# Attention scores of 32 tiles: two products over 64 rows into two PSUM banks in place of a block-diagonal product over 128 rows

## Chip, cores and metric

One core of one Trainium2 chip runs the whole program. The metric is the device time of one execution in microseconds (us). Of the kernel before there are three timed runs; of one more execution there is a profile, read below.

## What is computed

A pooled attention and two feed-forward layers with different activations, one after the other, in float32:

```python
# q, k, v: [B=8, H=8, S=576, D=64]
k_p = k.reshape(B, H, 72, 8, D).mean(axis=3)         # the same for v
scores = (1 / sqrt(D)) * q @ k_p.T                   # [B, H, 576, 72]
attn = softmax(scores)                               # along the 72
x = (attn @ v_p), heads side by side                 # [4608, 512]
h = x @ w_in                                         # [4608, 2048]
g = where(h >= 1, h, where(h <= -1, 0, (h + 1)**2 / 4))
x2 = g @ w_out                                       # [4608, 512]
out = relu(x2 @ w_in2)**2 @ w_out2                   # [4608, 512]
```

## The kernel before

The 4608 tokens are cut into 36 tiles of 128 (the attention's unit) and 9 blocks of 512 (the unit of the feed-forward layers). A batch has 576 tokens, which is four and a half tiles, so tiles 4, 13, 22 and 31 hold the end of one batch and the start of the next; they are called crossing tiles here. The eight heads of a tile are four pairs (`NP`), and a pair's 2 x 64 dimensions fill 128 rows.

**The attention of a tile** goes through units, each a few TensorE (PE) instructions and an evacuation. For tiles 4 to 35:

- `unit_q` gives the transposed queries `qT` (128 rows of a pair's dimensions, 4 pairs, 128 tokens); from tile 8 on the DVE transposes them and PE has no part in it.
- `unit_s` makes the scores, in two units per tile, `("s", t, 0)` and `("s", t, 1)`, each of two pairs. `kbd` holds the pooled keys of a batch as a block diagonal: rows 0 to 63 hold the first head of the pair in columns 0 to 71, rows 64 to 127 the second head in columns 72 to 143, and the rest is zero. One product of 128 rows and 144 columns (line 371) thus gives both heads of a pair. A crossing tile takes two products per pair, one for each batch, with 64 tokens each. The evacuation takes the maximum (line 389) and subtracts it (line 396) on the DVE; the exponential (line 411) runs on ACT a little later.
- `norm` (lines 429 to 440) sums and scales; the result goes out to DRAM and comes back in another order (`do_stores`, `fetch`), and the DVE turns it (`turn`, line 477) into `aT`.
- `unit_x` multiplies `aT` with the pooled values (line 487) into `px`; ACT and the DVE evacuate it as `xhi` (line 499) and `xlo` (line 500).

A float32 product appears as two passes on PE, each with its own weight load (PEld).

**The feed-forward work** runs in steps. Step `s` is `gemm1(s)` (12 products of 512 columns, line 665), then `gemm2(s - 2)` (12 of 512 columns, line 737; in the first ten steps 4 float32 ones, line 726), with the evacuations and weight splits on ACT and the DVE.

**What sets the order.** The table `slots` gives each unit a place: slot `2s` is between `gemm1(s)` and `gemm2(s - 2)`, slot `2s + 1` behind `gemm2`. For tiles 8 to 35, four steps apart, `("s", t, 0)` stands at `2c`, `("s", t, 1)` at `2c + 2` (one step later) and `("x", t)` at `2c + 11`; for tiles 4 to 7 the two score units stand at `2c` and `2c + 1`, in the same step. The recording layer then orders the instructions of each engine.

**PSUM.** Outside the opening, `bank` takes from the pool `ps_a`, which has two banks. All units of the attention share these two in turn; a unit waits until the bank's earlier user is evacuated. The products of `gemm1` and `gemm2` have banks of their own.

Of the kernel before, what the change touches and what calls it, by code (L numbers as in the profile page):

```python
# [10 lines left out]
F32 = mybir.dt.float32  # L11
# [3 lines left out]
AF = mybir.ActivationFunctionType  # L15
ALU = mybir.AluOpType
AX = mybir.AxisListType
# [16 lines left out]
def pooled_attention_moe_moe(  # L34
# [11 lines left out]
    nc = tc.nc  # L46
    B, H, S, D = q.shape
# [3 lines left out]
    SP = S // POOL  # L51
    P = 128
    NP = H // 2
# [6 lines left out]
    exp_scale = 1.0 / (POOL * float(D) ** 0.5)  # L60
# [17 lines left out]
    at = attn.enter_context(tc.tile_pool(name="at", bufs=2))  # L78
# [10 lines left out]
    kbd = [ac.tile([P, NP, 2 * SP], F32, name=f"kbd{i}") for i in range(2)]  # L89
# [10 lines left out]
    def runs(t0, n):  # L100
        done = 0
        while done < n:
            b, s = divmod(t0 + done, S)
            step = min(n - done, S - s)
            yield done, step, b, s
            done += step
# [119 lines left out]


    q_t, kv_t, kp, vp, qT, pn_t, p_d, z_t, aT = {}, {}, {}, {}, {}, {}, {}, {}, {}
    x_t, sums = {}, {}
    early, later, norms, stores, fetches, fetched, turns = [], [], [], [], [], [], []  # L230

    def bank(shape, name):

        n = early[-1] % 8 if early else 0
        if n >= 4:
            return ps_acc.tile(shape, F32, tag=f"acc{n - 4}", name=name)
        if n % 2:
            return ps_h.tile(shape, F32, tag="h", name=name)
        return ps_a.tile(shape, F32, tag="a", name=name)
# [102 lines left out]
    def unit_q(t):  # L342
# [20 lines left out]

        return evac

    def unit_s(t, g):
        pss = bank([P, 2, 2 * SP], "pss")
        for i in range(2):
            p = 2 * g + i
            for off, n, b, _ in runs(t * P, P):  # L370
                nc.tensor.matmul(  # L371
                    out=pss[off:off + n, i, :], lhsT=qT[t][:, p, off:off + n], rhs=kbd[b % 2][:, p, :],
                    start=True, stop=True,
                )
        if g == 0:
            if t == 3:
                pn = [gp.tile([P, H // 2, SP], F32, tag="gl", name="pn") for _ in range(2)]
            else:
                pn = early_pn(t) if t < 2 else at.tile([P, H, SP], F32, tag="pn", name="pn", bufs=1)
                pn = [pn[:, 0:H // 2, :], pn[:, H // 2:, :], pn]  # L380
            pn_t[t] = pn, at.tile([P, H, 1], F32, tag="mx", name="mx", bufs=4)
            if t in ON_ACT:
                sums[t] = at.tile([P, H, 1], F32, tag="sm", name="sm", bufs=4)
        pn, mx = pn_t[t][0][g], pn_t[t][1]
        h = slice(4 * g, 4 * g + 4)
        s4 = pss.rearrange("p i (e s) -> p (i e) s", e=2)

        def evac():
            nc.vector.tensor_reduce(out=mx[:, h, :], in_=s4, axis=AX.X, op=ALU.max)
            if t in ON_ACT:  # L390
                nc.vector.tensor_scalar(
                    out=mx[:, h, :], in0=mx[:, h, :], scalar1=-exp_scale, scalar2=None, op0=ALU.mult
                )
                later.append(exp)
                return
            nc.vector.tensor_tensor(
                out=pn, in0=s4, in1=mx[:, h, :].to_broadcast([P, 4, SP]), op=ALU.subtract
            )
            later.append(exp)

        def exp():
            if t in ON_ACT:
                for i in range(4 * g, 4 * g + 4):
                    nc.scalar.activation(
                        out=pn[:, i - 4 * g, :], in_=s4[:, i - 4 * g, :], func=AF.Exp, scale=exp_scale, bias=mx[:, i, :],
                        accum_out=sums[t][:, i, :],
                    )
                if g == 1:
                    norms.append(t)
                return  # L410
            nc.scalar.activation(out=pn, in_=pn, func=AF.Exp, scale=exp_scale)
            if g == 1:
                norms.append(t)

        return evac

    def early_pn(t):
        flat = pad[t].rearrange("p n h c -> p (n h c)")
        return flat[:, 0:H * SP].rearrange("p (h s) -> p h s", h=H)
# [87 lines left out]
    TB0 = TB // P  # L507
# [6 lines left out]
    for t in range(TB0, NTILE):  # L514
# [10 lines left out]
        if t in first_tile:  # L525
            b = first_tile.index(t)
# [36 lines left out]
    def unit(u):  # L563
        if u[0] == "k":
            b, p = u[1:]
            pool_to(b * 2 * NP + p + 2)
            return unit_k(b, p)
        if u[0] == "v":
            b, p = u[1:]
            pool_to(b * 2 * NP + NP + p + 2)  # L570
            return unit_v(b, p)
        if u[0] == "q":
            load_q_to(u[1] + (1 if u[1] >= TB0 else 0))
            return unit_q(u[1])
        if u[0] == "s":
            return unit_s(*u[1:])
        if u[0] == "p":
            return unit_p(*u[1:])
        b = max(r[2] for r in runs(u[1] * P, P))
        pool_to((b + 1) * 2 * NP)  # L580
        return unit_x(u[1])
# [295 lines left out]
    for u in before:  # L877
        op, args = u.rstrip("0123456789,"), [int(i) for i in u.lstrip(ascii_lowercase).split(",") if i]
# [220 lines left out]
    for n, u in enumerate(units):  # L1099
        kind, b, i, g = u  # L1100
# [52 lines left out]
```

## Time and profile before

| | |
|---|---|
| three timed runs | 1636.98, 1637.51, 1638.68 us |
| their median | 1637.51 us |
| span of the profiled execution (first to last instruction) | 1636.0 us |
| the rest of the median around that span | 1.51 us |
| PE busy | 1612.2 us (99% of the span), 7824 instructions |
| weight loads (PEld) busy | 1311.6 us (80%) |
| DVE busy | 1263.0 us (77%) |
| ACT busy | 893.5 us (55%) |
| chain that ended last | PE 91%, DVE 4%, DMA 2% |

The profiled execution has no time of its own beside its span; the median of the runs lies 1.51 us above it. A busy PE counts each product from its start to the end of its last column on the way out, so products that overlap are counted once, and the distance between the starts of two products tells more of what one costs than its duration does.

### The profile page before, as it was taken

The page shows a single profiled execution, that of the slowest core. Times are in us where ns is not written, and L with a number is a line of the kernel's source. Part 1 is how long each engine was busy: PE and PEld are TensorE (multiplying, and loading weights), DVE is VectorE, ACT ScalarE, POOL GpSimd, SP SyncE. Part 2 cuts the span into 40 slices and gives each one's busy share as a digit, 9 for nine tenths or more (in the row PEclk, how much of TensorE's full clock was granted, in tenths as well). Part 3 has the DMA queues.
Part 4 walks back from the last instruction along what each step waited for, and adds up shares of the span by engine and source line. Part 5 has one row for each costly group of instructions (what it writes and reads, how often), then busy time and mean ns, then how long its engine had stood idle before and what let it go on. Part 6 is the DMA issues. An engine that isn't in the chain of part 4 may idle for free.

```text
span 1636.0 us, 23310 instructions
## 1 busy us (share of the span) xinstructions
PE 1612.2 (99%) x7824; PEld 1311.6 (80%) x7824; DVE 1263.0 (77%) x2228; ACT 893.5 (55%) x1610; POOL 106.6 (7%) x75
## 2 busy tenths in 40 slices
PE   7999999999999999999999999999999999999998
PEld 6757888888878888888888888888888888888886
DVE  6998889998898999998884542579558855975585
ACT  6665556666666666666675532345335533553353
POOL 1442000011001000000100000000000000000000
PEclk9999999999999999999999999999999999999999
DMA  9664335544455554544470384667776776768675
GB/s 246 191 193 124 107 69 170 163 157 139 148 145 156 155 144 134 171 142 151 141 258 7 103 277 147 194 218 207 195 254 219 209 235 208 211 198 245 194 206 129
DMA packets 280518, 284.69 MB, mean 174 GB/s; under 512 B 154960, under 2 KB 183632, under 8 KB 280400
## 3 DMA queue, kind: packets, MB, share of 16 engines
q1 hardware_dynamic: 280400, 283.21, 58.0%
q8 instruction: 62, 1.02, 0.3%
q14 instruction: 56, 0.46, 0.1%
HBM read 218.10 MB, written 65.01 MB: 173 GB/s over the span
## 4 chain that ended last, share of the span: by engine, by line
PE 91%; DVE 4%; DMA 2%; ACT 1%; issue 1%; SPq 1%; POOL 0%; DVEq 0%; ACTq 0%; POOLq 0%
PE ph L665 25%; PE acc L737 25%; PE dp L1011 11%; PE cp L1002 10%; PE dq L1011 5%; PE cr L1002 5%; PE dr L1011 3%; PE cq L1002 2%; PE pss L371 2%; PE px L487 2%; DMA w<-w2i 1%; PE acc L726 1%; DVE wi L155 0%; DMA kv<-in_k_dram 0%; SPq L1068 0%
## 5 line engine op out<-in xcount | busy, mean ns | idle before, releaser
L665 PE MATMUL ph<-xhi,wihi 128*128 128x512 f32 x576 | 230.4, 400 | 1.4 <-ACT xhi L499 1.4
L665 PE MATMUL ph<-xlo,wihi 128*128 128x512 f32 x576 | 225.4, 391 | 0.0
L665 PE MATMUL ph<-xhi,wilo 128*128 128x512 f32 x576 | 225.2, 391 | 0.0
L959 ACT ACTIVATE gh<-g 128x512 fp32r<-128x512 f32 x224 | 139.5, 630 | 152.1 <-DVE g L1028 48.0
L737 PE MATMUL acc<-gh,wohi 128*128 128x512 f32 x536 | 215.8, 403 | 0.0
L737 PE MATMUL acc<-gl,wohi 128*128 128x512 f32 x536 | 209.5, 391 | 0.0
L737 PE MATMUL acc<-gh,wolo 128*128 128x512 f32 x536 | 209.0, 390 | 0.0
L767 DVE TENSOR_TENSOR gl<-g,gh 128x512 fp32r<-128x512 f32 x224 | 151.1, 686 | 47.6 <-ACT gh L959 46.2
L1002 PE MATMUL cp<-x,w 128*128 128x512 f32 x768 | 186.2, 390 | 0.2
L1002 PEld LDWEIGHTS cp<-x,w 128*128 128x128 f32 x768 | 143.9, 188 | 31.3 <-ACT s L1024 1.4
L1011 PE MATMUL dp<-gh,w 128*128 128x512 f32 x512 | 161.5, 389 | 0.0
L219 ACT ACTIVATE wihi<-wi 128x512 fp32r<-128x512 f32 x144 | 90.4, 628 | 125.3 <-PE ph L665 122.3
L223 DVE TENSOR_TENSOR wilo<-wi,wihi 128x512 fp32r<-128x512 f32 x144 | 105.3, 731 | 49.0 <-ACT wihi L219 47.7
L665 PEld LDWEIGHTS ph<-xhi,wihi 128*128 128x128 f32 x576 | 108.4, 188 | 28.5 <-issue 3.1
L665 PEld LDWEIGHTS ph<-xhi,wilo 128*128 128x128 f32 x576 | 108.5, 188 | 23.3 <-issue 0.2
L665 PEld LDWEIGHTS ph<-xlo,wihi 128*128 128x128 f32 x576 | 108.5, 188 | 22.0 <-issue 0.5
L700 ACT ACTIVATE gh<-g 128x512 fp32r<-128x512 f32 x134 | 84.2, 629 | 68.7 <-DVE g L698 68.1
L1024 ACT ACTIVATE s<-cp 128x512 f32<-128x512 f32 x96 | 57.1, 595 | 117.9 <-PE cp L1002 117.1
L706 DVE TENSOR_TENSOR gl<-g,gh 128x512 fp32r<-128x512 f32 x150 | 104.8, 698 | 18.6 <-ACT gh L700 15.9
L737 PEld LDWEIGHTS acc<-gl,wohi 128*128 128x128 f32 x536 | 100.6, 188 | 22.4
L737 PEld LDWEIGHTS acc<-gh,wohi 128*128 128x128 f32 x536 | 100.7, 188 | 20.3 <-issue 1.0
L737 PEld LDWEIGHTS acc<-gh,wolo 128*128 128x128 f32 x536 | 100.8, 188 | 19.5
(142 smaller groups left out, 3006.8 us busy)
## 6 DMA issues: line engine op xcount, KB each, us to landing
w<-w2i SPq DMA_DIRECT2D x224, 256.0 KB
w<-w2o SPq DMA_DIRECT2D x224, 256.0 KB
w2i<-cb SPq DMA_DIRECT2D x32, 512.0 KB
w2o<-cb SPq DMA_DIRECT2D x32, 512.0 KB
st<-in_moe_w_out_dram SPq DMA_DIRECT2D x31, 512.0 KB
st<-in_moe_w_in_dram SPq DMA_DIRECT2D x29, 512.0 KB
pd<-pad SPq DMA_DIRECT2D x32, 384.0 KB
z<-pd SPq DMA_DIRECT2D x96, 128.0 KB
```

Of the source, the lines that this page charges most:

```text
L219: nc.scalar.activation(out=hi, in_=src, func=AF.Copy)
L223: eng.tensor_tensor(out=lo, in0=src, in1=hi.bitcast(F32), op=ALU.subtract)
L371: nc.tensor.matmul(out=pss[off:off + n, i, :], lhsT=qT[t][:, p, off:off + n], rhs=kbd[b % 2][:, p, :], start=True, stop=True,)
L665: nc.tensor.matmul(out=ph, lhsT=a[:, kk % a.shape[1], :], rhs=c[:, kk, :], start=(i == 0), stop=(i == 3 * KD - 1))
L700: act(out=gh, in_=g, func=AF.Copy)
L706: nc.vector.tensor_tensor(out=gl, in0=g, in1=gh.bitcast(F32), op=ALU.subtract)
L737: nc.tensor.matmul(out=o, lhsT=lhsT, rhs=rhs, start=(f == 0 and x == 0), stop=(f == KF - 1 and x == 2),)
L767: tt(out=out, in0=a, in1=b, op=ALU.subtract)
L959: act(out=hi, in_=a, func=AF.Copy)
L1002: nc.tensor.matmul(out=out[0], lhsT=w[:, a, k, :], rhs=xq[b, i][c][:, k, :], start=(n == 0 and i in (1, 2, 7)), stop=(n == 5), skip_group_ ...
L1011: nc.tensor.matmul(out=out[d], lhsT=w[:, a, d, :], rhs=x[c], start=(g == 0 and n == 0 and i in (1, 2, 7, 4)), stop=(g == NG - 1 and n == 2 ...
L1024: act(out=snaps[key], in_=a, func=AF.Copy)
```

## The change

For tiles 4 to 35, `unit_s` hands over to a new function, `unit_rows`. Its first call (`e == 0`) takes both banks of `ps_a` and issues the products of all four pairs: for each pair and each batch one product over rows 0 to 63 (first head, into the first bank) and one over rows 64 to 127 (second head, into the second bank), each with 72 columns. The zero blocks of `kbd` are no longer read. The evacuation of a call takes one bank, with the heads of one row half; its output is strided. The second call (`e == 1`) issues no products and evacuates the other bank. Tiles 0 to 3, `slots` and all the rest stay.

```diff
+    def unit_rows(t, e):
+        if e == 0:
+            halves_s[t] = [bank([P, NP, SP], "pss") for _ in range(2)]
+            for p in range(NP):
+                for off, n, b, _ in runs(t * P, P):
+                    for i, o in enumerate(halves_s[t]):
+                        d = slice(i * D, (i + 1) * D)
+                        nc.tensor.matmul(
+                            out=o[off:off + n, p, :], lhsT=qT[t][d, p, off:off + n],
+                            rhs=kbd[b % 2][d, p, i * SP:(i + 1) * SP], start=True, stop=True,
+                        )
+            pn = at.tile([P, H, SP], F32, tag="pn", name="pn", bufs=1)
+            pn_t[t] = [None, None, pn], at.tile([P, H, 1], F32, tag="mx", name="mx", bufs=4)
+        src = halves_s[t][e]
+        pn, mx = (a.rearrange("p (i e) s -> p e i s", e=2)[:, e] for a in (pn_t[t][0][2], pn_t[t][1]))
+        if e == 1:
+            halves_s.pop(t)
+
+        def evac():
+            nc.vector.tensor_reduce(out=mx, in_=src, axis=AX.X, op=ALU.max)
+            nc.vector.tensor_tensor(out=pn, in0=src, in1=mx.to_broadcast([P, NP, SP]), op=ALU.subtract)
+            later.append(exp)
+
+        def exp():
+            nc.scalar.activation(out=pn, in_=pn, func=AF.Exp, scale=exp_scale)
+            if e == 1:
+                norms.append(t)
+
+        return evac
+
     def unit_s(t, g):
+        if t >= TB0:
+            return unit_rows(t, g)
         pss = bank([P, 2, 2 * SP], "pss")
```

Lines behind the new function stand 32 further down in the changed kernel: 665 is 697 there, 737 is 769 and 500 is 532.

How this moves instructions, at three places. **PE, step 24** (the first score unit of tile 11; `ph` is `gemm1`, `acc` is `gemm2`, `pss` the scores). Before:

```order
L665 MATMUL ph<-xhi,wihi 128x512
L665 MATMUL ph<-xlo,wihi 128x512
L665 MATMUL ph<-xhi,wilo 128x512
L371 MATMUL pss<-kbd_118,qT 128x144 x2
L737 MATMUL acc_1874<-gh,wohi 128x512
L737 MATMUL acc_1874<-gh,wolo 128x512
L737 MATMUL acc_1874<-gl,wohi 128x512
```

Now:

```order
L697 MATMUL ph<-xhi,wihi 128x512
L697 MATMUL ph<-xlo,wihi 128x512
L697 MATMUL ph<-xhi,wilo 128x512
L373 MATMUL pss<-kbd_118,qT 128x72 x8
L769 MATMUL acc_1902<-gh,wohi 128x512
L769 MATMUL acc_1902<-gh,wolo 128x512
L769 MATMUL acc_1902<-gl,wohi 128x512
```

Eight products of 72 columns, of the two row halves by turns, stand where two of 144 stood. **PE, step 25** (where the second score unit of tile 11 stood). Before:

```order
L665 MATMUL ph<-xhi,wihi 128x512
L665 MATMUL ph<-xlo,wihi 128x512
L665 MATMUL ph<-xhi,wilo 128x512
L371 MATMUL pss<-kbd_118,qT 128x144 x2
L737 MATMUL acc_1874<-gh,wohi 128x512
L737 MATMUL acc_1874<-gh,wolo 128x512
L737 MATMUL acc_1874<-gl,wohi 128x512
```

Now:

```order
L697 MATMUL ph<-xhi,wihi 128x512
L697 MATMUL ph<-xlo,wihi 128x512
L697 MATMUL ph<-xhi,wilo 128x512
L769 MATMUL acc_1902<-gh,wohi 128x512
L769 MATMUL acc_1902<-gh,wolo 128x512
L769 MATMUL acc_1902<-gl,wohi 128x512
```

`gemm2` follows `gemm1` with nothing between them. **DVE, about step 8** (the rows up to `xlo`, the evacuation of tile 4's `px`, and behind it; `kv` and `kp` pool the keys, `wi` and `wo` are weights under conversion). Before:

```order
L297 TENSOR_TENSOR kv<-kv 72x2x256
L223 TENSOR_TENSOR wilo<-wi_898,wihi 128x512
L698 SCALAR_TENSOR_TENSOR gw<-ph,u 128x512
L297 TENSOR_TENSOR kv<-kv 72x2x128
L158 TENSOR_SCALAR wi_1162<-wi_1162 128x512
L298 TENSOR_TENSOR kp<-kv 72x128
L161 SCALAR_TENSOR_TENSOR wi_1162<-st,wi_1162 128x512
L155 TENSOR_SCALAR wo_1254<-wo_1254 128x512
L158 TENSOR_SCALAR wo_1254<-wo_1254 128x512
L161 SCALAR_TENSOR_TENSOR wo_1254<-st,wo_1254 128x512
L500 TENSOR_TENSOR xlo<-px,xhi 128x4x128
```

Now:

```order
L155 TENSOR_SCALAR wi_1178<-wi_1178 128x512
L158 TENSOR_SCALAR wi_1178<-wi_1178 128x512
L730 SCALAR_TENSOR_TENSOR gw<-ph,u 128x512
L161 SCALAR_TENSOR_TENSOR wi_1178<-st,wi_1178 128x512
L155 TENSOR_SCALAR wo_1270<-wo_1270 128x512
L158 TENSOR_SCALAR wo_1270<-wo_1270 128x512
L161 SCALAR_TENSOR_TENSOR wo_1270<-st,wo_1270 128x512
L532 TENSOR_TENSOR xlo<-px,xhi 128x4x128
L223 TENSOR_TENSOR wolo<-wo_1270,wohi 128x512
L509 STREAM_TRANSPOSE aT<-z 96x1024
L223 TENSOR_TENSOR wilo<-wi_971,wihi 128x512
L385 TENSOR_REDUCE mx<-pss 128x4 x2
```

The three pooling instructions that stood ahead of `xlo` stand behind it now.

## Rows read from the trace of the kernel before

**Rows 1.** The page: busy time by engine, and the chain that ended last.

```profile
PE 1612.2 (99%) x7824; PEld 1311.6 (80%) x7824; DVE 1263.0 (77%) x2228; ACT 893.5 (55%) x1610; POOL 106.6 (7%) x75
PE 91%; DVE 4%; DMA 2%; ACT 1%; issue 1%; SPq 1%; POOL 0%; DVEq 0%; ACTq 0%; POOLq 0%
```

**Rows 2.** Busy time in two stretches: length, PE, PEld, DVE, ACT, POOL, PEclk, DMA.

```profile
41.00:164.00 123.00, 118.28 (x674) 83.44 (x673) 117.11 (x205) 75.95 (x143) 46.17 (x28) 1.00 0.60 169
164.00:800.00 636.00, 636.00 (x3238) 519.48 (x3237) 569.76 (x1097) 408.94 (x748) 46.87 (x28) 1.00 0.48 144
```

**Rows 3.** Timeline of PE, tiles 25 and 26: start, duration, line, count.

```profile
549.65 0.65 PE L371 MATMUL pss<-kbd,qT 128*128 128x144 f32 x4
...
565.58 0.39 PE L665 MATMUL ph<-xhi,wihi 128*128 128x512 f32 x1
...
571.02 0.39 PE L665 MATMUL ph<-xhi,wihi 128*128 128x512 f32 x1
...
573.74 0.65 PE L371 MATMUL pss<-kbd,qT 128*128 128x144 f32 x4
579.72 0.65 PE L371 MATMUL pss<-kbd,qT 128*128 128x144 f32 x4
```

**Rows 4.** Timeline of PE, the two score units of crossing tile 13.

```profile
258.23 0.71 PE L371 MATMUL pss<-kbd,qT 128*64 128x144 f32 x8
...
264.57 0.71 PE L371 MATMUL pss<-kbd,qT 128*64 128x144 f32 x8
```

**Rows 5.** Timeline of PE, a `px` unit between regular products.

```profile
582.75 0.39 PE L737 MATMUL acc<-gl,wohi 128*128 128x512 f32 x1
583.07 1.09 PE L487 MATMUL px<-aT,vp 72*64 72x128 f32 x16
584.10 0.50 PE L665 MATMUL ph<-xhi,wihi 128*128 128x512 f32 x1
584.43 0.40 PE L665 MATMUL ph<-xlo,wihi 128*128 128x512 f32 x1
```

**Rows 6.** Timeline of the weight loads (PEld) there.

```profile
583.07 0.85 PEld L487 LDWEIGHTS px<-aT,vp 72*64 72x64 f32 x16 [0.35 <-issue]
584.09 0.19 PEld L665 LDWEIGHTS ph<-xhi,wihi 128*128 128x128 f32 x1 [0.17 <-issue]
584.20 0.19 PEld L665 LDWEIGHTS ph<-xlo,wihi 128*128 128x128 f32 x1
```

**Rows 7.** Groups by line and form: count, busy us, mean ns.

```profile
L371 PEld LDWEIGHTS pss<-kbd,qT 128*128 128x128 f32 x256 | 39.8, 193 | 7.4 <-DVE xlo L500 1.8 <-issue 0.7 <-ACT qT L362 0.4
L371 PEld LDWEIGHTS pss<-kbd,qT 128*64 128x64 f32 x64 | 3.7, 136 | 4.4 <-issue 3.3 <-ACT kbd L319 0.7 <-ACT pn L411 0.4
```

**Rows 8.** Timeline of PE, 32 passes of 72 columns in two column halves.

```profile
57.76 1.22 PE L309 MATMUL pk<-ident,kv 72*64 72x72 f32 x32
58.91 0.50 PE L665 MATMUL ph<-xhi,wilo 128*128 128x512 f32 x1
```

**Rows 9.** Groups by line and form: a score unit's maximum on the DVE.

```profile
L389 DVE TENSOR_REDUCE mx<-pss 128x4 f32<-128x288 f32 x72 | 32.3, 449 | 3.0 <-PE pss L371 2.9
```

**Rows 10.** Timeline of PE, then of DVE, around the scores of tile 6.

```profile
103.19 0.65 PE L371 MATMUL pss<-kbd,qT 128*128 128x144 f32 x4
103.68 3.60 PE L726 MATMUL acc<-gw,wo 128*128 128x512 f32 x8
108.21 0.76 PE L371 MATMUL pss<-kbd,qT 128*128 128x144 f32 x4 [0.93 <-DVE xlo L500]
...
112.99 0.30 PE L355 MATMUL pq<-ident,q 128*128 128x128 f32 x1 [1.28 <-issue]
102.15 1.38 DVE L298 TENSOR_TENSOR kp<-kv 72x128 f32<-72x128 f32 x1
...
107.47 0.68 DVE L500 TENSOR_TENSOR xlo<-px,xhi 128x512 fp32r<-128x512 f32 x1
```

**Rows 11.** Waits of PE between 41 and 164 us: total us, times, longest.

```profile
PE px L487 <- DVE aT L477: 1.3, 2, 1.1
```

More of the change, by code (lines that the diff above doesn't have):

```diff
@@ L228, in pooled_attention_moe_moe @@
     q_t, kv_t, kp, vp, qT, pn_t, p_d, z_t, aT = {}, {}, {}, {}, {}, {}, {}, {}, {}
-    x_t, sums = {}, {}
+    x_t, sums, halves_s = {}, {}, {}
     early, later, norms, stores, fetches, fetched, turns = [], [], [], [], [], [], []
```

## Prediction

> **What bounds the kernel.** The page comes first: PE is busy for 99% of the span and makes 91% of the chain that ended last [rows 1]. The scores lie in the first half, so the second view is busy time by stretch. From 164 to 800 us PE is busy in 636.00 of 636.00 us: it waits for nothing, and what the change adds to PE there, or takes off, is added to the end. From 41 to 164 us PE has 4.7 us of idle time and the DVE is busy in 117.11 of 123 [rows 2]; there both engines are near the bound and waits decide. The third view is the timeline of PE, where distances between starts give prices.
>
> A step without any unit takes 571.02 - 565.58 = 5.44 us (24 products, 0.227 each). From the first score unit of tile 26 to its second is 5.98, so **a score unit costs 0.54**. Tile to tile takes 573.74 - 549.65 = 24.09, that is four steps (21.76), two score units (1.08) and one `px` unit, which so costs 1.25 [rows 3]. In a crossing tile a score unit costs 264.57 - 258.23 - 5.44 = 0.90 [rows 4]. A tile's scores thus cost 1.08, or 1.80 in a crossing tile.
>
> **Where the price of a unit on half the array comes from.** `px` is the nearest relative of the new unit: 16 passes that run by twos on two halves of the array, column halves there, row halves in the change. Three things make its 1.25. Its first load comes 0.32 after the last regular product's start in place of 0.23: nothing is loaded ahead, PE empties first. From its first load to the next regular load is 1.02, with 0.17 of idle at the end, in which PE empties again; the rest, 0.85, is 8 pairs of passes at 0.107. Then 0.11 for a weight load that nothing covers [rows 5, 6]. The score units of regular tiles pay none of this: they are full-array products, and their loads run ahead.
>
> **The change, part by part.**
>
> *Removed:* two score units per tile, 1.08 regular, 1.80 crossing.
>
> *Added:* one unit of 16 passes (8 products, two passes each), by twos on the two row halves. A pass streams 72 columns: 32 such passes in pairs took 58.91 - 57.76 = 1.15, less 0.17 for emptying, which is 0.061 per pair [rows 8]. But each pass wants its own load of 128 columns, and two loads that follow each other at once stand 0.11 apart [rows 6]; 64 columns take 57 ns less [rows 7], so a load goes by columns, about 0.83 ns each. Before, a load of 0.107 hid under a stream of 0.12 (144 columns); now it is longer than the stream of 0.061 and sets the pace. How loads of two row halves stand to each other no row shows. From below: they run side by side, as those of two column halves do, and a pair costs 0.107, or at best the stream's 0.061. From above: one after the other, 0.214. I take 0.107, since the column halves are the nearest row. The unit is then `px` over again, 8 pairs at 0.107 and the same two emptyings: **1.25, against 1.08: +0.17 for each of 28 regular tiles, +4.8**.
>
> The Trainium skill speaks against the change at this point: "TensorE: Matmul & The Clock Gate", section LDWEIGHTS, says that a load goes by its columns alone, and that one of 32 rows takes as long as one of 128. By that halving the rows saves nothing on a load, and the sum stays as it is; no row here has a load of 64 rows.
>
> *Crossing tiles* 4, 13, 22 and 31: loads of 64 columns (0.057) and streams of 72 (0.061), on four quarters. With all four side by side 8 slots at 0.061 make 0.49 in place of `px`'s 0.86, so 1.25 - 0.37 = 0.88 in place of 1.80: -0.92 for each of 4 tiles, **-3.7**.
>
> *Evacuation:* the same two maxima, subtractions and exponentials per tile, of the same sizes. The DVE now has both maxima in one step, 0.45 us and a subtraction earlier than before [rows 9]. It is busy in 90% of that stretch and PE waited for it nowhere [rows 2]; I cost this at nothing. Without that cover it would be at most 0.9 per tile, 25 us in all, and `g` and `gl` would come late for `gemm2`.
>
> *Waits in the steady stretch:* the unit wants both banks of `ps_a` at once. Their last users are the scores of the tile before and the `px` unit of two tiles before, some two steps (11 us) earlier; I cost this at nothing.
>
> *Waits in the early stretch.* In tiles 4 to 7 the units stand closer. At tile 6 PE reaches the scores at 103.19; the bank that `px` of tile 4 holds comes free with `xlo` at 107.47 + 0.68 = 108.15. Before, the second unit alone needed it, with 3.60 of `gemm2` ahead of it, and PE waited 0.93. Now the second product needs it and `gemm2` is queued behind: with the same `xlo` PE waits about 4.8, 3.9 more. Against this: the pooling of keys is moved behind `xlo`, and its last instruction alone took 1.38; the wait of 1.28 at 112.99, for the bank of the scores, falls on a later PE [rows 10]; so do the 1.3 of waits for `aT` [rows 11]. From +3.9 down to 3.9 - 1.38 - 1.28 - 1.3 = -0.1, and below that to -1.3, if the wait for the bank doesn't grow. I take **+1.0**, nearer to the lower end, since three rows pull that way.
>
> *The sum:* 4.8 - 3.7 + 1.0 = **+2.1**. On the profiled span of 1636.0 that is 1638.1; the median of the runs lies 1.51 above the span, so **1639.6**. By its bounds (a pair between 0.102 and 0.112, which is 1.1 either way; early waits between -1.3 and +3.9) this case goes from 1636.2 to 1643.6. A measurement of this kernel can tell about 0.2%, 3.3 us; the forecast is within it.
>
> **Rivals.**
>
> *One after the other (slower).* Place: the loads of the 28 regular units. If the two row halves load through one door by turns, a pair costs 0.214, the unit 2.11, +1.03 x 28 = +28.8; a crossing unit 8 x 0.122 = 0.98, so 1.37, -0.43 x 4 = -1.7; with +1.0 for the waits **1665.6**. For it: halves of columns have separate columns, halves of rows share them. Against it: loads and products of column halves go side by side without loss. It decides early: from a pair of 0.112 on the change is slower by over 0.2%.
>
> *No load ahead (slower).* If a half can't load its next weights while it multiplies, a pair costs 0.107 + 0.061 = 0.168, the unit 1.73, +18.2; a crossing unit 8 x 0.118 = 0.94, so 1.33, -1.9; with the waits **1654.8**. Against it: `px` loads under its products; its pairs would cost 0.16 otherwise.
>
> *The stream alone counts (faster).* If loads of 64 rows are short, or hide, a pair costs 0.061 and the unit 0.88: -0.20 x 28 = -5.6, crossing -3.7, waits +1.0: **1629.3**. About the same comes out if the row halves need no emptying. Against it: the loads' 0.11 and the idle 0.17 [rows 6]. The Trainium skill has this as a rule: "TensorEngine Tiling (Array Packing)", section Theoretical Speedup, gives up to twice the speed where the contraction is 64 or less. Halving the 8 passes of 0.12 of a tile's two units gives the same 0.48. The traces bear it out for the streams alone, so its chance is small.
>
> *The change does not do what it says:* if PE treats the halves as full-array products, with no pairs, that is the first rival's price less the emptyings, and shares its chance.
>
> **How the numbers follow.** Side by side at the load's pace: 0.58, of which 0.40 within 0.2%, 0.13 slower, 0.05 faster. One after the other: 0.16. No load ahead: 0.08. The stream alone: 0.12. Early waits outside their bounds: 0.06 (0.02 within, 0.03 slower, 0.01 faster). So faster 0.18, within 0.2% 0.42, slower 0.40. The range takes in the first, the third and the fourth case, 1629 to 1655, and leaves out the second.
>
> **What would show it.** Right: in the changed profile the 16 passes of a unit start by twos, 0.107 apart, with 0.17 of idle loads behind them; tile to tile takes about 24.26 in place of 24.09, and crossing tiles 0.9 less than before; PE stays busy throughout from 164 to 800. Wrong: starts one by one, pairs of 0.06 or 0.17, loads that start while PE still streams the products before the unit, or waits of PE for the DVE in the steady stretch. A longer wait for `xlo` at tile 6 belongs to the forecast; one of more than 5 us does not.

## The result, and the profile after

The changed kernel takes 1650.77 us (median of four runs, 1649.55 to 1652.80) against 1638.10 for the kernel before (four runs, 1636.98 to 1639.27): **1.0068 times as long, 95% interval 1.0055 to 1.0082**. The two medians lie 12.7 us apart, 0.77%, which that interval takes in. The forecast was 1639.6, within 0.2% of no change. The time lies inside the stated range, but 7 us above the upper end of the likeliest case (1643.6), and nearer to a rival's figure (1654.8) whose mechanism did not happen.

The profiled execution took 1651.62 (span 1649.8). In the changed kernel the lines behind the new function are 32 higher: the scores are line 373, `px` 519, `xlo` 532, `gemm1` 697, `gemm2` 769 and 758. Busy time by stretch first, beside [rows 2], and three short windows of the early stretch (columns as there; PEclk is the third from the end):

```profile
41.00:164.00 123.00, 117.40 (x696) 81.27 (x695) 116.03 (x199) 73.19 (x137) 41.01 (x29) 0.96 0.58 169
164.00:800.00 636.00, 632.52 (x3439) 512.07 (x3438) 563.41 (x1091) 402.68 (x744) 49.05 (x28) 1.00 0.48 142
...
105.00:110.00 5.00, 2.49 (x18) 2.20 (x18) 3.43 (x5) 1.25 (x3) 2.56 (x2) 0.82 0.85 227
110.00:115.00 5.00, 5.00 (x7) 1.90 (x7) 5.00 (x11) 4.06 (x9) 0.00 (x0) 0.50 0.18 29
115.00:120.00 5.00, 5.00 (x22) 3.48 (x21) 5.00 (x12) 2.47 (x5) 1.34 (x1) 1.00 0.47 140
```

Two things are new. From 164 to 800 us PE is idle for 3.5 us, where it never was, and the early stretch has a mean clock of 0.96, with 0.50 from 110 to 115: TensorE ran there at 1.2 GHz in place of 2.4. The waits of PE (total us, times, longest) name the places:

```profile
PE pss L373 <- ACT kbd L319: 3.4, 4, 1.3
PE pss L373 <- DVE xlo L532: 2.5, 1, 2.5
PE pq L355 <- issue: 1.9, 1, 1.9
```

**The price of the unit** is read where nothing waits: PE's timeline around a regular tile, the weight loads there (and all loads of regular units as a group: count, busy us, mean ns), and PE at crossing tile 31.

```profile
584.83 0.39 PE L697 MATMUL ph<-xhi,wilo 128*128 128x512 f32 x1
585.15 1.11 PE L373 MATMUL pss<-kbd,qT 64*128 64x72 f32 x16
586.20 0.50 PE L769 MATMUL acc<-gh,wohi 128*128 128x512 f32 x1
586.53 0.39 PE L769 MATMUL acc<-gh,wolo 128*128 128x512 f32 x1
```

```profile
585.15 0.97 PEld L373 LDWEIGHTS pss<-kbd,qT 64*128 64x128 f32 x16 [0.35 <-PE ph L697]
586.20 0.19 PEld L769 LDWEIGHTS acc<-gh,wohi 128*128 128x128 f32 x1
...
L373 PEld LDWEIGHTS pss<-kbd,qT 64*128 64x128 f32 x448 | 28.7, 190 | 13.6 <-PE ph L697 7.8 <-DVE xlo L532 2.7 <-issue 1.4
```

```profile
707.59 0.39 PE L697 MATMUL ph<-xhi,wilo 128*128 128x512 f32 x1
707.90 0.73 PE L373 MATMUL pss<-kbd,qT 64*64 64x72 f32 x32
708.57 0.50 PE L769 MATMUL acc<-gh,wohi 128*128 128x512 f32 x1
708.91 0.40 PE L769 MATMUL acc<-gh,wolo 128*128 128x512 f32 x1
```

From the regular product before to the second one behind, 586.53 - 584.83 = 1.70; without the unit it would be 2 x 0.227, so the unit costs **1.25**, as forecast. Its 16 loads start by twos, 6 ns apart: eight pairs in 0.97 us, the last load being 0.19 long, are (0.97 - 0.19) / 7 = 0.111 apart. The crossing unit costs 708.91 - 707.59 - 0.45 = 0.87, forecast 0.88. Tile to tile takes 24.28 where nothing waits:

```profile
191.27 1.11 PE L373 MATMUL pss<-kbd,qT 64*128 64x72 f32 x16
...
215.55 1.11 PE L373 MATMUL pss<-kbd,qT 64*128 64x72 f32 x16
```

That is +0.19 on the 24.09 of [rows 3]; +0.17 was forecast. A crossing tile gives back 0.9.

**The early stretch**, PE's timeline at tile 6, beside [rows 10]:

```profile
105.01 0.44 PE L373 MATMUL pss<-kbd,qT 64*128 64x72 f32 x2
107.96 1.79 PE L373 MATMUL pss<-kbd,qT 64*128 64x72 f32 x14 [2.51 <-DVE xlo L532]
109.68 6.34 PE L758 MATMUL acc<-gw,wo 128*128 128x512 f32 x8
```

The first two passes run, then PE waits 2.51 us for the second bank. Behind that the granted clock is at its lower level, and the eight `gemm2` passes take 6.34 us, in place of 3.60 [rows 10]. The wait at `pq` of tile 5 has no releaser in the view (`issue`); it ends at 64.01, 0.1 us after the first of these two subtractions on the DVE, which empties the first bank of tile 4's scores:

```profile
63.46 0.81 DVE L386 TENSOR_TENSOR pn<-pss,mx 128x288 f32<-128x288 f32 x2
```

**The steady stretch**, PE at tiles 18 and 22 (three of the four waits; the fourth, 0.47, is at tile 13):

```profile
386.91 0.44 PE L373 MATMUL pss<-kbd,qT 64*128 64x72 f32 x2
388.07 1.11 PE L373 MATMUL pss<-kbd,qT 64*128 64x72 f32 x14 [0.72 <-ACT kbd L319]
...
486.71 0.34 PE L373 MATMUL pss<-kbd,qT 64*64 64x72 f32 x2 [0.97 <-ACT kbd L319]
488.33 0.72 PE L373 MATMUL pss<-kbd,qT 64*64 64x72 f32 x30 [1.28 <-ACT kbd L319]
```

Tiles 13, 18 and 22 are the first to use a new batch's keys (so are 4, 9, 27 and 31; of these only 27 lost time here, 0.46 us with 0.03 of waiting). These come through two `k` units at slots `2c - 2` and `2c - 1`, and ACT copies each into `kbd` (lines 318 and 319). Before, pairs 2 and 3 were wanted only at `2c + 2`, one step later; the one unit wants all four at `2c`. The kernel before used that step: at tile 18 its last copy ended at 380.25, after the first score unit had started (the second started at 385.79).

```profile
379.96 0.29 ACT L319 ACTIVATE kbd<-pk 64x144 f32<-64x144 f32 x1
379.81 0.65 PE L371 MATMUL pss<-kbd,qT 128*128 128x144 f32 x4
```

In the changed kernel, ACT at tile 22 shows why the copies are late (first the last of the PE products that they copy, line 314):

```profile
482.63 0.29 PE L314 MATMUL pk<-ident,kp 72*128 72x72 f32 x2
...
480.04 0.63 ACT L174 ACTIVATE cb<-z 128x512 fp32r<-128x512 f32 x1 [3.45 <-POOL z L164]
...
484.03 0.63 ACT L174 ACTIVATE cb<-z 128x512 fp32r<-128x512 f32 x1 [1.24 <-DVE z L201]
...
486.09 0.27 ACT L318 ACTIVATE kbd<-pk 64x144 f32<-64x144 f32 x1
...
487.99 0.28 ACT L319 ACTIVATE kbd<-pk 64x144 f32<-64x144 f32 x1
```

The products were done at 482.92, their copies ran at 487.69 and 487.99, behind what stands before them in ACT's order. A conversion of second-layer weights (`cb`) had held ACT for 3.45 us until POOL was done, another for 1.24; what stood behind them came late, the copies of `kbd` with it.

**Three places on the way.** The start of three `px` units divides the span: tile 0 (in the opening), tile 9 (end of the close tiles) and tile 35 (the last). In the kernel before they start at 27.25, 194.76 and 824.54 us, in the changed one at 28.23, 200.71 and 837.18. The changed kernel is thus 0.98 late at the first, loses 4.97 to the second (the *early shift*) and 6.69 to the third (the *steady shift*); what follows adds 1.2. The 0.98 is no effect of the change: E4 and E12 below, which alter nothing that early, are 1.26 and 1.28 late there.

### The profile page after: what moved, and what is told of

Same layout as the page of the kernel before. It is cut to its first block, busy times and chain, and to the rows that moved or that the text cites. A ratio compares the mean times of both kernels' runs of the same rounds, so it can differ in the third digit from the quotient of the medians.

```text
span 1649.8 us, 23897 instructions
## 1 busy us (share of the span) xinstructions
PE 1620.5 (98%) x8112; PEld 1312.4 (80%) x8112; DVE 1260.6 (76%) x2228; ACT 889.5 (54%) x1610; POOL 102.9 (6%) x75
## 4 chain that ended last, share of the span: by engine, by line
PE 83%; DVE 8%; DMA 3%; ACT 2%; issue 1%; SPq 1%; POOL 1%; DVEq 0%; POOLq 0%; ACTq 0%
PE ph L697 22%; PE acc L769 21%; PE dp L1043 11%; PE cp L1034 10%; PE dq L1043 5%; PE cr L1034 5%; PE dr L1043 3%; PE cq L1034 2%; PE px L519 2%; PE pss L373 2%; PE acc L758 1%; DMA kv<-in_k_dram 1%; POOL z L164 1%; SPq L255 1%; DMA st<-in_moe_w_in_dram 1%
## 5 line engine op out<-in xcount | busy, mean ns | idle before, releaser
L769 PE MATMUL acc<-gh,wohi 128*128 128x512 f32 x536 | 212.2, 396 | 0.0
L799 DVE TENSOR_TENSOR gl<-g,gh 128x512 fp32r<-128x512 f32 x224 | 151.5, 688 | 47.8 <-ACT gh L991 46.2
L223 DVE TENSOR_TENSOR wilo<-wi,wihi 128x512 fp32r<-128x512 f32 x144 | 99.9, 694 | 38.7 <-ACT wihi L219 38.3
L738 DVE TENSOR_TENSOR gl<-g,gh 128x512 fp32r<-128x512 f32 x150 | 108.1, 721 | 25.4 <-ACT gh L732 22.9
```

The costliest lines, as they stand in the source:

```text
L223: eng.tensor_tensor(out=lo, in0=src, in1=hi.bitcast(F32), op=ALU.subtract)
L738: nc.vector.tensor_tensor(out=gl, in0=g, in1=gh.bitcast(F32), op=ALU.subtract)
L769: nc.tensor.matmul(out=o, lhsT=lhsT, rhs=rhs, start=(f == 0 and x == 0), stop=(f == KF - 1 and x == 2),)
L799: tt(out=out, in0=a, in1=b, op=ALU.subtract)
```

## The experiments

The theory: the price of the units is near the forecast, some 2 us, and the rest is waits that come with *one unit per tile*, early for the second bank, later for `kbd`. Rivals: the rows themselves bring waits and clock; the DVE is what is waited for. Each run has its ratio to the kernel before with the 95% interval, and the two shifts of its profile as defined above. Where the text gives a ratio in us, it is its distance from 1 (or from another ratio) times 1638.

| run | ratio | early shift, us | steady shift, us |
|---|---|---|---|
| E1 early_old | 1.0040 (1.0025 to 1.0056) | +2.61 | +5.24 |
| E2 k_earlier | 1.0053 (1.0037 to 1.0070) | +4.96 | +1.59 |
| E3 both | 1.0022 (1.0012 to 1.0031) | +3.32 | +1.59 |
| E4 cross_only | 0.9984 (0.9975 to 0.9993) | +0.04 | -2.66 |
| E5 before_k_earlier | 1.0004 (0.9995 to 1.0013) | +1.65 | 0.00 |
| E6 early_only | 1.0044 (1.0032 to 1.0056) | +6.72 | 0.00 |
| E7 merge_alone | 1.0017 (1.0008 to 1.0026) | +9.54 | -1.81 |
| E7b merge_late | 0.9996 (0.9987 to 1.0005) | +2.39 | -1.81 |
| E8 halves_in_turn | 1.0100 (1.0086 to 1.0114) | +2.92 | +13.79 |
| E10 tile6_later | 1.0059 (1.0046 to 1.0073) | +5.81 | +2.16 |
| E11 change_again | 1.0081 (1.0065 to 1.0098) | +4.89 | +4.70 |
| E12 best_of_both | 0.9981 (0.9971 to 0.9990) | -0.03 | -3.54 |

The early shift of one profile is good to some 2 us only: E5 alters nothing there and shows +1.65 (its rows, further down, say why). The steady shift repeats to a hundredth where nothing waits.

**E2, the keys earlier.**

```diff
-            todo.update({2 * c - 2 + i // 2: ("k", b, i) for i in (0, 2)})
+            todo.update({2 * c - 2 - (t > 9) + i // 2: ("k", b, i) for i in (0, 2)})
```

> The change, with the two k units of batches 3 to 7 (tiles 13 to 31) one slot earlier (2c-3 and 2c-2 in place of 2c-2 and 2c-1). Theory: the four waits of the scores for kbd (5.1 us over a bare unit) go, as all four pairs are evacuated half a step before the unit; the time is the changed kernel's less 4.5 to 5.5 us, some 1645.5, with units of 0.87 us (crossing) and 1.25 us at tiles 13, 18, 22, 27. Rival: what is waited for is the DVE, whose two maxima and two subtractions come closer together, and kbd is only the last of several; then the waits stay under another name and the time changes by under 1.5 us.

Measured: the waits for `kbd` are gone, PE is busy throughout again, and the steady shift falls from 6.69 to 1.59, by 5.10.

```profile
164.00:800.00 636.00, 636.00 (x3464) 515.02 (x3464) 566.12 (x1096) 405.72 (x749) 49.05 (x28) 1.00 0.48 145
```

With the DVE's work unchanged, the DVE as the cause falls in this stretch. The 1.59 is the bare price of 25 tiles, read from `px` to `px` against the kernel before: 22 x 0.193 - 3 x 0.887. Against it the changed kernel loses 0.79 at tile 13, 1.19 at 18, 2.65 at 22 and 0.46 at 27, more than the 3.4 of the waits by themselves. In the ratios the gain is smaller, 1.0068 to 1.0053, 2.5 us (4.6 us against E11's 1.0081), and the intervals overlap; E11 shows that these waits differ between executions.

**E1, early tiles as before**, and **E3, both edits.**

```diff
-        if t >= TB0:
+        if t >= 2 * TB0:
             return unit_rows(t, g)
```

> Tiles 4 to 7 keep their two block-diagonal units; tiles 8 to 35 as in the change. Theory: the stretch up to tile 9's scores lost 5.65 us in the changed kernel (wait for xlo in tile 6's unit with the half clock behind it, and the wait at pq of tile 5). All of that goes, so the time is the changed kernel's less 5 to 6 us, some 1645, and the clock stays at 1.00 from 41 to 164 us. Rival: the rows' products themselves bring the lower clock and the loss, wherever they start; then it comes up at the first tiles behind tile 8 and the time stays within 2 us of the changed kernel's.

> Both edits: tiles 4 to 7 as before, k units one slot earlier. Theory: only the bare price of the units is left against the kernel before, 25 tiles by +0.195 and 3 crossing tiles by -0.92, +2.1 us: some 1640, between 0 and 4 above the kernel before. Rival: there is a further loss in the steady stretch that the two waits hide; then it stays 5 us or more above the kernel before.

Measured: E1 gained 4.6 us (1.0068 to 1.0040) and its clock from 105 to 164 us stayed at 1.00. Part of that gain is that its profile waits less for `kbd` (steady shift 5.24 in place of 6.69); E3 against E2, where neither waits for `kbd`, is the cleaner pair, 1.0053 to 1.0022, 5.1 us. E3 is 3.6 us above the kernel before, within what was expected of it. Of its early shift 1.4 is a wait at tile 4's second score unit (2.2 in place of 0.8), which the edit leaves as it was. And it has one new wait of 2.0 us at `px` of tile 6, which comes behind the two maxima and subtractions of tile 8, the first tile that has the one unit there:

```profile
PE px L519 <- DVE pn L386: 2.0, 1, 2.0
```

**E6, the early tiles alone** have the new unit (`TB0 <= t < 2 * TB0`).

> Rows and one unit for tiles 4 to 7 alone, two old units for tiles 8 to 35. Theory: the early loss by itself, the wait in tile 6's unit, the half clock behind it and the waits at pq and px: 4 to 6 us over the kernel before, some 1643.5. Rival: what is lost up to tile 9 is made good by work that the DVE and the DMAs get ahead with in the meantime; then it is within 2 us of the kernel before.

Measured: 1.0044, 7.2 us, above the 4 to 6 expected, and nothing of it is made good later (steady shift 0.00). The early tiles cost more than half of the whole loss, and the rival falls.

**E7, one unit without rows.** In `unit_rows` the products are the old ones, all four pairs in one unit:

```diff
+                    nc.tensor.matmul(
+                        out=halves_s[t][p // 2][off:off + n, p % 2, :], lhsT=qT[t][:, p, off:off + n],
+                        rhs=kbd[b % 2][:, p, :], start=True, stop=True,
+                    )
```

> Half of the change: one unit per tile for tiles 4 to 35, all four block-diagonal products over 128 rows in two PSUM banks, no split by rows; k units where they were. Theory: the waits come from the one unit, not from the rows. A merged unit costs 8 passes of 0.122 us (the spacing of the old unit's four, 555.634 to 555.999), 0.98 as the two old ones did, so nothing is gained or lost by it, and the waits for kbd (some 5 us) and the loss up to tile 9 (some 5.6 us, with the wait for xlo in tile 6's unit and the half clock behind it) are there as in the change: some 10.5 us over the kernel before, 1649 to 1650. Rival: the products of 64 rows bring the waits and the lower clock; then there is no half clock behind tile 6, and the time is within 3 us of the kernel before.

Measured: 3 us over the kernel before, far from the 10.5 expected, and so by its time nearer to the rival. Its trace speaks against the rival all the same:

```profile
105.00:110.00 5.00, 4.71 (x49) 3.81 (x48) 5.00 (x8) 3.36 (x6) 2.52 (x2) 1.00 1.07 292
110.00:115.00 5.00, 0.31 (x1) 0.32 (x2) 4.86 (x8) 1.92 (x4) 2.23 (x3) 0.79 0.87 215
115.00:120.00 5.00, 5.00 (x10) 2.59 (x10) 5.00 (x9) 1.86 (x4) 0.45 (x1) 0.53 0.18 29
```

```profile
109.06 0.65 PE L371 MATMUL pss<-kbd,qT 128*128 128x144 f32 x4
114.69 1.33 PE L371 MATMUL pss<-kbd,qT 128*128 128x144 f32 x4 [4.98 <-DVE xlo L530]
115.81 5.55 PE L756 MATMUL acc<-gw,wo 128*128 128x512 f32 x8
```

With no product of 64 rows in its scores, the unit of tile 6 waits for `xlo` in its middle and the clock falls behind it, as in the change. But that execution is the slowest of its eleven, 1645.93 against a median of 1641.85, with a mean granted clock of 0.992 where the other ten have 0.995 or 0.996. It has another such wait, at tile 4, and the clock at 0.50 behind it:

```profile
PE pss L371 <- DVE pn L384: 3.1, 1, 3.1
60.00:65.00 5.00, 5.00 (x30) 3.05 (x29) 4.90 (x6) 0.88 (x2) 2.64 (x2) 0.50 0.95 287
```

So its early shift of 9.54 is not that of a usual run, and no trace shows the other ten. Their times do: E7 is 3.4 us over E7b below, whose early tiles are as before and whose steady shift is the same. The early tiles thus cost 3.4 us without rows, 5.1 with them (E2 against E3); whether the rows add the difference is open. What the theory missed is the other half: E7 hardly waits for `kbd` (0.2 us in all, at tile 27, where it loses 0.45), although its keys are where the change has them, and it gains in the steady stretch. A merged regular tile is 24.05 apart (0.04 less than before), a crossing one is 0.46 cheaper:

```profile
438.12 1.14 PE L371 MATMUL pss<-kbd,qT 128*128 128x144 f32 x8
...
462.17 1.14 PE L371 MATMUL pss<-kbd,qT 128*128 128x144 f32 x8
```

**E11, the change once more**, in a series of its own.

> The change itself, unaltered, on one chip with the next three. Theory: the waits for kbd depend on where ACT's queue stands (its copies of kbd come behind conversions that wait for POOL) and so differ from execution to execution; the times spread over 3 us or more and another profile shows the waits at other tiles or of other lengths, while the wait for xlo in tile 6's unit (2.5 us) and the half clock behind it stay. Rival: the waits are fixed by the order of the program; then the profile repeats 3.4 us in four waits at tiles 13, 18, 22 and 27.

Measured: the wait for `xlo` (2.3) and the half clock (0.76 and 0.56 from 105 to 115) are there again. The profile's waits for `kbd` are not the same:

```profile
PE pss L373 <- ACT kbd L319: 1.7, 2, 1.0
```

Over a bare unit they cost 4.70 - 1.59 = 3.1 us here against 5.1 in the first profile, and in E1 (two waits, at tiles 13 and 31) 3.65 by the same difference. The program is the same, so they do not follow from its order alone; that it is where ACT's queue stands is argued from the rows at tile 22. Why E7 has almost none is open: its last copies end from 0.5 us before the start of the unit to 0.8 after it, in the change up to 2.5 after, and one profile can't tell a milder cause from luck.

**E10, tile 6 half a step later.**

```diff
+        if t == 6:
+            todo = {at_s1: ("s", t), at_x: ("x", t)}
...
+        if u == ("s", 6):
+            both = [unit_s(6, g) for g in range(2)]
+            return lambda: [f() for f in both]
```

> As e2_k_earlier, with tile 6's unit half a step later (slot 17, both evacuations there). Theory: at slot 17 the second bank is 0.9 us from free (as the second unit in the kernel before), so the wait of 2.5 us in the middle of tile 6's unit shrinks to about 1, the clock stays at 1.00 behind it, and the eight products behind take 3.6 us in place of 6.3: 4 to 5 us less than e2_k_earlier, some 1644. Rival: the half clock is the rows' doing, or follows any wait in this stretch; then the clock still falls between 105 and 115 us and the gain is under 2 us.

Measured: no gain over E2. The wait for `xlo` is gone, but another one took its place, and the clock fell behind that one (0.70 from 120 to 125):

```profile
118.48 0.63 PE L355 MATMUL pq<-ident,q 128*128 128x128 f32 x4 [4.15 <-issue]
118.94 5.29 PE L763 MATMUL acc<-gw,wo 128*128 128x512 f32 x8
```

`pq` of tile 7 stands right behind, and now finds both banks held until the DVE has evacuated tile 6. So the loss does not hang on the place of this one unit: two banks taken at once leave none for the next unit while the DVE is behind.

**E8, halves in turn**, E3 with the loop over `i` outside that over `p`.

> As e3_both, but within a unit all products of rows 0 to 63 first and then all of rows 64 to 127. Theory: what makes sixteen half products cost little more than eight whole ones is that a load and a product of one half go beside those of the other; in this order successive ones share their rows, each pass takes at least the 0.112 us that a pair takes now, and a regular unit grows by 8 times 0.112 = 0.9 us or more: 25 regular tiles and 3 crossing ones of twice as many passes, some 25 to 30 us over e3_both. Rival: PE takes half products at that rate in any order, as their 72 columns are short, or the scheduler puts them back side by side; then it is within 2 us of e3_both.

Measured: 12.2 us of steady shift over E3, less than half of the 25 to 30 expected. A unit takes 190.62 - 189.07 = 1.55 to the next product, 1.05 in the change:

```profile
189.07 1.62 PE L373 MATMUL pss<-kbd,qT 64*128 64x72 f32 x16
190.62 0.50 PE L769 MATMUL acc<-gh,wohi 128*128 128x512 f32 x1
```

The side-by-side run of the two halves is what keeps the unit at 1.25, but eight passes of 0.112 more would be 0.9, and 0.5 came: the second half's loads start while the first half is still at work (its first at 189.58, the first half's last at 189.85), so the halves overlap in part in this order too.

**E5**, the kernel before with E2's edit, **E4**, rows at tiles 13, 22 and 31 alone (`t in (13, 22, 31)`, with E2's edit), **E7b**, E7 for `t >= 2 * TB0` with E2's edit, and **E12**: rows at 13, 22 and 31, E7's unit for the other tiles from 10 on, E2's edit.

> The kernel before, with only the k units of batches 3 to 7 one slot earlier. Theory: nothing waits for kbd there, so the move is worth nothing: within 1 us of the kernel before. Rival: the gain of the three crossing tiles alone (2.9 us) was in part the k units' new place; then this one is 1 us or more faster.

> Rows only for the crossing tiles 13, 22 and 31, all other tiles with the two old units; k units of batches 3 to 7 one slot earlier. Theory: three tiles by -0.92 us, -2.8 us against the kernel before, some 1635.3, a gain of 0.17 percent. Rival: a switch to rows costs at a single tile what it costs at every tile and the k units' new place costs as well; then the time is the kernel before's within 1 us, or above.

> One block-diagonal unit of four pairs over 128 rows for tiles 8 to 35, tiles 4 to 7 as before, k units one slot earlier: e3_both without the split by rows. Theory, from the merged units of e7_merge_alone (-0.04 us per regular tile, -0.46 per crossing one against the two old units): 25 by -0.04 and 3 by -0.46, -2.4, and with it the waits at tile 8 that e3_both showed (some +2): about the kernel before, within 2 us, and 4 us less than e3_both. Rival: the merged unit brings the steady stretch waits of its own; then it is 3 us or more over the kernel before.

> Rows for the crossing tiles 13, 22 and 31, one block-diagonal unit over 128 rows for the other tiles from 10 on, two old units for tiles 0 to 9, k units one slot earlier. Theory: 3 by -0.92 and 23 by -0.04, -3.7 us against the kernel before and 1 less than e4_cross_only: some 1634.5 to 1636. Rival: two banks held by every tile bring waits in the steady stretch that the two units did not have; then it is no faster than e4_cross_only (0.9984 of the kernel before).

Measured: all four as expected. E5 is the same as the kernel before. Its early shift of 1.65 is a wait of 1.2 us for a DMA of values, ending at 78.30, and the lower clock behind it, at a place that its edit does not touch:

```profile
PE pv L328 <- DMA kv<-in_v_dram: 1.2, 1, 1.2
80.00:85.00 5.00, 5.00 (x23) 4.33 (x22) 3.64 (x5) 0.92 (x3) 1.99 (x2) 0.74 0.83 271
```

**E4 and E12 are faster than the kernel before, by 2.6 and 3.1 us**, under 0.2%, but with intervals that end below 1; the two can't be told apart by time, but in the steady shifts E12 has 0.88 more, 22 x 0.04. PE in E12 (busy time by stretch) waits nowhere in the steady stretch:

```profile
164.00:800.00 636.00, 636.00 (x3311) 521.59 (x3312) 578.72 (x1110) 410.00 (x754) 47.13 (x29) 1.00 0.49 144
```

E7b against E3 is the price of the rows by itself: the steady shift differs by 1.59 + 1.81 = 3.4 us, or 3.85 without the 0.45 that E7b loses at tile 27 to a wait for `kbd`.

## Why the prediction was right and wrong

- **The stated range: it held by luck.** It reached up to 1655 for "No load ahead", with a pair at 0.168; pairs stand 0.111 apart. Waits brought the time there, which the sum had at +1.0 in all. The outcome with the best chance, within 0.2%, did not come. "PE stays busy throughout from 164 to 800" failed, and the sign of being wrong had the DVE as the engine that PE waits for; it was ACT.
- **The unit on half the array: right.** 1.25 forecast, 1.25 measured, with pairs 0.111 apart in place of 0.107 and somewhat less idle time at its end. Loads of 64 rows took 190 ns on the mean, those of 128 rows 193 [rows 7]; so the price is set by loads that are as long as before under streams half as long. The Trainium skill's rule that a load goes by its columns alone ("TensorE: Matmul & The Clock Gate", section LDWEIGHTS) agrees with these two means. The Trainium skill's other figure, up to twice the speed ("TensorEngine Tiling (Array Packing)", section Theoretical Speedup), is an upper bound that a regular tile came nowhere near: it became dearer, 1.25 in place of 1.08. Only in crossing tiles, where loads have 64 columns, did the halves gain 0.9. That `px` was so good a model is in part chance: its loads have 64 columns and its streams 128 [rows 5, 6], so its pace is, as an estimate from [rows 8], that of the streams (0.061 x 128 / 72 = 0.108); in the new unit it is that of the loads, of as many columns.
- **Regular tiles +4.8 and crossing tiles -3.7: right, a little low.** E2 and E3 show it alone: 0.193 and -0.887 per tile, +5.4 and -3.5. "One after the other", "no load ahead" and "the stream alone" did not happen.
- **"Waits in the steady stretch ... I cost this at nothing": wrong, 3 to 5 us.** The step looked at the two banks and their last users. It did not look at the unit's other operand: by merging two units, pairs 2 and 3 of `kbd` are wanted a step earlier, and the copies that make them come late in ACT's order for the step before. The prediction's own [rows 7] held a hint: the loads of the crossing tiles had stood idle for 0.7 us until `kbd` was copied (line 319). The banks were indeed free.
- **"Evacuation ... I cost this at nothing": right in the steady stretch.** E2 has both maxima in one step and PE waits nowhere. Where tiles stand closer it was not: E3's `px` waits 2.0 behind the DVE's work for tile 8.
- **"Waits in the early stretch, +1.0, between -1.3 and +3.9": the term was mis-sized; it is 5 to 7 us** (early shift 4.97; 7.2 us by time in E6), outside its bounds. The wait for `xlo` was 2.51, inside the bounds, and the 1.28 at 112.99 did go. Two things were left out. One is the lower clock behind a wait: 6.34 - 3.60 = 2.7 us for the eight passes behind it, and 1.79 - 1.11 = 0.7 for the unit's own 14 passes. The other is the same shortage of banks at another unit, the 1.93 at `pq` of tile 5 that the kernel before did not have. With 1.6 more at `xlo` (2.51 - 0.93) and 1.3 less at 112.99 that makes 2.7 + 0.7 + 1.9 + 1.6 - 1.3 = 5.6; smaller waits of the kernel before that went, 0.8 at tile 4's scores and 1.3 for `aT` [rows 11], and a new one of 0.9 at `px` of tile 6 bring it to 4.4, and the rest of the 4.97 is not accounted for. On the banks the Trainium skill has a warning that the prediction passed over: tiling by rows raises the pressure on PSUM, as different row tiles write to different banks ("TensorEngine Tiling (Array Packing)", section Gotcha 1: PSUM Pressure). The 2.51 and 1.93 agree with it, but E7 shows that a merged unit of whole rows pays as well, so here it is the merging that takes both banks.
- **"A wait for xlo of more than 5 us does not belong to the forecast": too lax as a sign.** Behind half of that the clock was at its lower level.

So the direction of the forecast's sum was right, its size was not: 1.9 us of price where 1.1 was worked out, and some 10 of waits in place of 1.

## What to carry to other kernels

When two units become one, list every operand and every buffer that the second one had a step longer to wait for, find the engine queue that produces each, and ask how late that queue can be; a full PE has no slack to hide it. Splitting these products by rows paid where a load (64 columns) is no longer than its stream (72), and not where it is longer (128); used in three crossing tiles alone it beat both kernels, by a little (E4). And the price of a wait of PE is not only its length: 2.51 us cost 3.4 more at the lower clock. Whether that comes can't be told from the length (next section), so work it into the bounds.

## What was not expected of the hardware

- A wait of 2.5 us (2.3 in E11, 4.98 in E7, 4.15 in E10) went with a stretch at the lower clock level, in the wait or behind it, whichever instruction waited; from 105 to 110 us PE had been busy for 2.49 us. The length of the wait does not decide it. The lower level also came behind 1.2 us at `pv` (E5, above) and 2.2 at `px` of tile 6 (E7b), while in E1 and E3 waits of 2.2 at tile 4's scores and of 2.0 at the same `px` left the clock at 1.00. No run isolates what does. The stretches with the wait of 2.2 at `px` in E7b, of 2.0 there in E3 and of 2.2 at tile 4 in E3:

```profile
140.00:145.00 5.00, 4.57 (x25) 3.66 (x26) 5.00 (x12) 2.42 (x5) 0.08 (x1) 0.66 0.45 110
...
140.00:145.00 5.00, 3.00 (x25) 2.19 (x24) 5.00 (x11) 2.03 (x5) 1.58 (x1) 1.00 0.58 169
...
55.00:60.00 5.00, 2.80 (x14) 1.30 (x14) 5.00 (x10) 2.92 (x6) 1.58 (x2) 1.00 0.94 279
```

- From 164 to 800 us the clock was 1.00 in every run.
- Loads of the two row halves go side by side, 0.111 us from one pair to the next with loads of some 0.19 each, as those of column halves do [rows 6].
- In E8 all loads of one half precede the other's in the program, and still the unit is 0.4 us shorter than eight passes more would make it.
